# Windowed attention cut into pieces of one 1024-position chunk instead of 342 positions of two chunks

## The chip, the cores and the metric

One core of a Trainium2 chip runs the whole kernel. The engines that matter are TensorE (PE in the profile, with its weight loads as PEld), ScalarE (ACT), VectorE (DVE), GpSimd (POOL), and SyncE (SP), whose queue issues nearly all DMA transfers. Each takes its own instructions in order and waits on semaphores for the others. The metric is the device time of one execution in microseconds.

## What is computed

The input x has 2048 positions of 1024 features; there are 32 heads of 32 features. Two attention blocks read the same x, and a gate per position mixes them.

```python
def _A_ref(x, wqkv, wo):          # linear attention
    ...
    phi = lambda t: jnp.where(t > 0, t + 1, jnp.exp(t)) + 1e-6
    pq, pk = phi(q), phi(k)
    kv = jnp.einsum("bhsd,bhse->bhde", pk, v)
    z = jnp.einsum("bhsd->bhd", pk)
    num = jnp.einsum("bhqd,bhde->bhqe", pq, kv)
    den = jnp.einsum("bhqd,bhd->bhq", pq, z)[..., None] + 1e-6
    o = num / den
    ...
def _B_ref(x, wqkv, wo):          # each position sees itself and 7 earlier ones, 2 apart
    W, dil = 8, 2
    ...
    idx = pos[:, None] - off[None, :]
    mask = idx >= 0
    ...
    logits = jnp.einsum("bhsd,bhswd->bhsw", q, kg) * scale
    logits = jnp.where(mask[None, None, :, :], logits, -1e9)
    attn = _softmax(logits, axis=-1)
    o = jnp.einsum("bhsw,bhswd->bhsd", attn, vg)
    ...
g = _sigmoid((x * gate_w).sum(-1, keepdims=True))
return g * _A_ref(x, A_wqkv, A_wo) + (1 - g) * _B_ref(x, B_wqkv, B_wo)
```

## The kernel before

**Parity.** Attention B steps by 2, so even and odd positions never meet. The kernel keeps them apart: parity p is 0 or 1, each with 1024 positions, and a window of 8 neighbours within its parity.

**Products.** All large matrix products (q, k, v of both blocks and the output projection) use a seven-product scheme in place of eight. The class `Group` computes four output tiles of 128x512 with the products m1 to m7. One product is four matmuls of 512 columns (eight in the output projection). `run` interleaves neighbouring groups: m1 and m2 of the new group, m3 of the one before, m6 of the new, m4 of the one before (`end_of`), then m7 and m5 of the new one. The products m1, m6, m5 and m3 accumulate in one PSUM tile X, one after another. After m1, m6 and m5, ACT saves what X holds so far (`save`, L261: tiles M1s, U2s, U4s), and the next of these products may write X only when that save has read it. The products m2, or m7 and m4, go to a PSUM tile Y; DVE adds the saved tile to it (`acc`, L234) and writes the result (kT, qT, tA, va, vA and so on). X and Y each exist twice, by the parity of the group. That is four PSUM banks.

**Side steps.** The other four banks are one single tile, `side_ps`, tag "s", one buffer. The attention of B (`attn`), the sum kv of block A (`kv`, tile kps) and the last part of A (`qa_out`, tile oA) take turns in it. They are generators: each `yield` gives a delay before the next step of that generator and a number of products for which no other side step may start. `side` counts the products and calls `step`, which takes the next step that is due. PE and SP follow this order as written. The order of ACT and DVE instructions comes out of a scheduler of the framework when the kernel is built; exps, Lns and the copies out of PSUM are marked high priority, and weight sums (L132 to L135) and the sums of phi (L521 to L523) are strewn between products by `defer`.

**Attention B.** For each of four groups of features (nn) and each parity there is one attention, eight in all. A group of features covers two chunks of 128 features (ch 0 and 1), four heads each (g). Positions go in blocks of QB = 57, because a block of 57 and the 7 before it fit in 64 keys. Blocks go in pairs, b = 0 and 1, on partitions 0 to 63 and 64 to 127. A piece t holds three pairs of both chunks, 6 x 57 = 342 columns, and the padded length SPAN is 3 x 342 = 1026. So there are three pieces per attention, 24 in all:

- `scores(t)`: 48 small matmuls (L672) into s, an exp on ACT into PT (L678), and a multiplication by the mask on DVE (L680).
- `pv(t, PT)`: 48 matmuls (L690) with the values and 8 with ones (L696) into o; on ACT, Ln of the row sums into rB (L702) and its exp with -1 (L704), which is the reciprocal; on DVE a copy of the sums into nB (L703) and the product oB (L706). oB is stored to OB_d (L707).

The steps are S0, S1, V0, S2, V1, V2, three products apart. nB and rB have one buffer, oB two. `load_v` reads the values from V_d, where `vb_store` has put them; `out_load` (L778, L781) reads OB_d and OA_d for the output projection.

**Block A beside it.** In the middle of the kernel row groups (`ka_group`, `va_group`) alternate with column groups (`k_group`, `q_group`). In `ka_group`, m3 ends with a cast tA on ACT (L232), followed by the exp eA (L520) and three sums on DVE. After the last kv step KVz is ready, and the queries of A (`qa_plain`, L635) with their oA steps follow.

Of the kernel before, what the change touches and what calls it, by code (L numbers as in the profile page):

```python
# [8 lines left out]
ACT = mybir.ActivationFunctionType  # L9
ALU = mybir.AluOpType  # L10
AX = mybir.AxisListType
BF16 = mybir.dt.bfloat16
FP16 = mybir.dt.float16
F32 = mybir.dt.float32
P = 128
QB = 57
NPAIR = 9
TW = 6 * QB
SPAN = 3 * TW
EPS = 1e-6  # L20
RATE_R = 0.8
OA_DELAY = 5
# [5 lines left out]
def kernel(  # L28
# [27 lines left out]

    consts = ctx.enter_context(tc.tile_pool(name="consts", bufs=1))
    dram = ctx.enter_context(tc.tile_pool(name="dram", bufs=1, space=bass.MemoryType.DRAM))
    V_d = [dram.tile([SPAN, D], BF16, name=f"V_d{p}") for p in range(2)]
    OB_d = [dram.tile([8, P, SPAN], BF16, name=f"OB_d{p}") for p in range(2)]  # L60
    OA_d = [[dram.tile([512, D], BF16, name=f"OA_d{p}{i}") for i in range(2)] for p in range(2)]

    chainp = ctx.enter_context(tc.tile_pool(name="chainp", bufs=5))
# [135 lines left out]

    maskp = consts.tile([P, 2, 6, QB], BF16, name="maskp")
    nc.gpsimd.memset(maskp[:, :, 0, :], 0.0)
    for w in range(8):
        for base in (7 - w, 71 - w):
            nc.gpsimd.affine_select(out=maskp[:, 0, 0, :], in_=maskp[:, 0, 0, :], compare_op=ALU.not_equal,
                                    fill=1.0, base=base, pattern=[[1, QB]], channel_multiplier=-1)
        nc.gpsimd.affine_select(out=maskp[0:64, 1, 0, :], in_=maskp[0:64, 1, 0, :], compare_op=ALU.not_equal,
                                fill=1.0, base=-w, pattern=[[1, QB]], channel_multiplier=-1)
    nc.gpsimd.tensor_copy(out=maskp[64:P, 1, 0, :], in_=maskp[64:P, 0, 0, :])  # L210
    for e in range(1, 6):
        nc.gpsimd.tensor_copy(out=maskp[:, 0, e, :], in_=maskp[:, 0, 0, :])
        nc.gpsimd.tensor_copy(out=maskp[:, 1, e, :], in_=maskp[:, 1 if e == 3 else 0, 0, :])
    ones = consts.tile([P, 32], BF16, name="ones")
    nc.gpsimd.memset(ones[:], 1.0)
    for p in range(2):
        nc.gpsimd.dma_start(out=V_d[p][1024:SPAN, :].rearrange("r (a e) -> (r a) e", e=P), in_=warm[0:16, 0:P])
    bd = consts.tile([P, 4, 33], F32, name="bd")
    nc.gpsimd.memset(bd[:], 0.0)
    for i in range(4):  # L220
# [105 lines left out]
    def col_ops(w, p):  # L326
        return lambda m, kc: (w.get(m, kc), xop(m, kc, p, slice(0, 512)))
# [18 lines left out]
    def step(force=False):  # L346
        seen = set()
        for entry in list(queue):
            if entry[4] in seen:
                continue  # L350
            seen.add(entry[4])
            if not force and (entry[0] > state["now"] or state["free"] > state["now"]):
                continue
            state["free"] = state["now"] + entry[3]
            try:
                delay, entry[3] = next(entry[1])
                entry[0] = state["now"] + delay
# [182 lines left out]
    def va_group(w, pair):  # L540
        vs = v_tiles("vA")

        def kv():
# [18 lines left out]
            if last:  # L562
                nc.vector.tensor_tensor(out=KVz[:].rearrange("p c (g e) -> p c g e", g=4),
                                        in0=KVacc[:, :, None, :].broadcast_to([P, 8, 4, 33]),
                                        in1=bd[:, None, :, :].broadcast_to([P, 8, 4, 33]), op=ALU.mult)
            yield 2, 2

        def done(i):
# [84 lines left out]
            f()  # L653


    def q_of(t, j, b):
        return TW * t + 2 * QB * j + QB * b

    def attn(nn, p, kT, qT, vw):

        def scores(t):
            s = side_ps("s")
            for ch in range(2):
                for j in range(3):
                    e = (3 * ch + j) * QB
                    for b in range(2):
                        q0 = q_of(t, j, b)
                        k0 = max(0, q0 - 7)  # L670
                        for g in range(4):
                            nc.tensor.matmul(s[64 * b:64 * b + 64, g, e:e + QB],  # L672
                                             lhsT=kT[32 * g:32 * g + 32, 1024 * ch + k0:1024 * ch + k0 + 64],
                                             rhs=qT[32 * g:32 * g + 32, 1024 * ch + q0:1024 * ch + q0 + QB],
                                             start=True, stop=True)
            PT = ptp.tile([P, 4, TW], BF16, name="PT", tag="PT")
            with tc.high_priority():
                nc.scalar.activation(out=PT[:], in_=s[:, :, 0:TW], func=ACT.Exp, scale=SCALE)  # L678
            m = maskp[:, 0 if t else 1, :, :].rearrange("p i q -> p (i q)")
            nc.vector.tensor_tensor(out=PT[:], in0=PT[:], in1=m[:, None, :].broadcast_to([P, 4, TW]), op=ALU.mult)  # L680
            return PT

        def pv(t, PT):
            o = side_ps("o")
            for e in range(6):
                ch, j = divmod(e, 3)
                for g in range(4):
                    for b in range(2):
                        rows = slice(64 * b, 64 * b + 64)
                        nc.tensor.matmul(o[32 * g:32 * g + 32, 2 * b, QB * e:QB * e + QB],  # L690
                                         lhsT=vw[rows, 3 * t + j, 4 * ch + g, :],
                                         rhs=PT[rows, g, QB * e:QB * e + QB], start=True, stop=True)
            for g in range(4):
                for b in range(2):
                    rows = slice(64 * b, 64 * b + 64)
                    nc.tensor.matmul(o[32 * g:32 * g + 32, 2 * b + 1, 0:TW], lhsT=ones[rows, :], rhs=PT[rows, g, :],  # L696
                                     start=True, stop=True)
            nB = ofp.tile([P, 2, TW], F32, name="nB", tag="nB", bufs=1)
            rB = ofp.tile([P, 2, TW], F32, name="rB", tag="rB", bufs=1)
            oB = ofp.tile([P, 6, 2, QB], BF16, name="oB", tag="oB", bufs=2)  # L700
            with tc.high_priority():
                nc.scalar.activation(out=rB[:], in_=o[:, 1:4:2, 0:TW], func=ACT.Ln)  # L702
                nc.vector.tensor_copy(out=nB[:], in_=o[:, 0:4:2, 0:TW])  # L703
            nc.scalar.activation(out=rB[:], in_=rB[:], func=ACT.Exp, scale=-1.0)  # L704
            num, r = (ap.rearrange("p b (e q) -> p e b q", e=6) for ap in (nB[:], rB[:]))
            nc.vector.tensor_tensor(out=oB[:], in0=num, in1=r, op=ALU.mult)  # L706
            nc.sync.dma_start(out=OB_d[p][2 * nn:2 * nn + 2, :, TW * t:TW * t + TW].rearrange("c p q -> p c q"),  # L707
                              in_=oB[:].rearrange("p (c j) b q -> p c (j b q)", c=2))

        last = None  # L710
        yield 0, 2
        for t in range(4):
            if t < 3:
                PT = scores(t)
                yield (1, 3) if last else (3, 3)
            if last:
                pv(*last)
                yield 1, 3
            last = (t, PT)

    def load_v(nn, p):
        vw = vwp.tile([P, NPAIR, 8, 32], BF16, name="vw", tag="vw")
        for b, j, n in ((0, 0, 1), (0, 1, 8), (1, 0, 9)):
            k0 = max(0, q_of(0, j, b) - 7)
# [5 lines left out]
    its = {}  # L730

    def k_group(w, nn, p):
        kT = kqp.tile([P, 2050], BF16, name="kT", tag="kq")
        nc.gpsimd.memset(kT[:, 2048:2050], 0.0)
        its[nn, p] = kT
        return Group(col_ops(w, p), lambda i, j, ps, add: acc(kT[:, 1024 * j + 512 * i:1024 * j + 512 * i + 512], ps, add))

    def q_group(w, nn, p):
        qT = kqp.tile([P, 2050], BF16, name="qT", tag="kq")
        nc.gpsimd.memset(qT[:, 2048:2050], 0.0)  # L740
# [5 lines left out]
        return Group(col_ops(w, p), lambda i, j, ps, add: acc(qT[:, 1024 * j + 512 * i:1024 * j + 512 * i + 512], ps, add), done)  # L746


    Wo = {}
# [230 lines left out]
```

## Time and profile before

| What | Value |
|---|---|
| Median of 4 executions | 463.56 us (463.48 to 464.62) |
| Profiled execution, its own time | 464.62 us |
| Its span, first to last instruction | 462.8 us |
| PE busy | 447.3 us (97%) |
| DVE busy | 285.9 us (62%) |
| ACT busy | 241.7 us (52%) |
| First score matmul to last score exp | 68.3 to 290.3 us |
| Exp of a piece (128x1368), 24 times | 1.31 us each |
| Mask product, 24 times | 0.87 us each |
| Ln, reciprocal, nB, oB, 24 times each | 0.74, 0.77, 0.87, 0.87 us each |

The profile lists busy time by engine and, in 40 slices of the span, the busy share in tenths. An instruction's row gives its line, engine, shapes and time. A busy time of PE is modelled from pipelined matmuls; some matmul records are missing, so that a product of four can show as "x3".

### The profile page before, as it was taken

The page shows a single profiled execution, that of the slowest core. Times are in us where ns is not written, and L with a number is a line of the kernel's source. Part 1 is how long each engine was busy: PE and PEld are TensorE (multiplying, and loading weights), DVE is VectorE, ACT ScalarE, POOL GpSimd, SP SyncE. Part 2 cuts the span into 40 slices and gives each one's busy share as a digit, 9 for nine tenths or more (in the row PEclk, how much of TensorE's full clock was granted, in tenths as well). Part 3 has the DMA queues.
Part 4 walks back from the last instruction along what each step waited for, and adds up shares of the span by engine and source line. Part 5 has one row for each costly group of instructions (what it writes and reads, how often), then busy time and mean ns, then how long its engine had stood idle before and what let it go on. Part 6 is the DMA issues. An engine that isn't in the chain of part 4 may idle for free. (4 is left out here: it accounts for less than half of the span.)

```text
span 462.8 us, 11887 instructions
## 1 busy us (share of the span) xinstructions
PE 447.3 (97%) x5060; PEld 218.5 (47%) x5137; DVE 285.9 (62%) x458; ACT 241.7 (52%) x367; POOL 56.7 (12%) x130
## 2 busy tenths in 40 slices
PE   8989999999999999999999999999998999999996
PEld 5435444444444454444444444445544444444444
DVE  0546578668848668486683846579875973154312
ACT  1223337558558485584865858536675645221221
POOL 8000000000000000000000000006675323000000
PEclk9989999999999999999999999999999999999999
DMA  8999721491120612206122065464229972699211
GB/s 178 194 226 237 260 51 64 124 270 25 37 49 18 154 23 57 43 18 144 33 53 48 17 137 175 124 177 113 68 73 202 183 171 79 120 177 182 68 47 45
DMA packets 117941, 51.65 MB, mean 112 GB/s; under 512 B 77696, under 2 KB 115840, under 8 KB 117888
## 3 DMA queue, kind: packets, MB, share of 16 engines
q1 hardware_dynamic: 117520, 50.62, 46.9%
q8 instruction: 40, 0.66, 0.6%
q10 hardware_dynamic: 272, 0.26, 0.2%
q0 software_dynamic: 96, 0.01, 0.1%
q14 instruction: 13, 0.11, 0.1%
HBM read 25.69 MB, written 16.79 MB: 92 GB/s over the span
## 5 line engine op out<-in xcount | busy, mean ns | idle before, releaser
L252 PEld LDWEIGHTS <-xT 128*128 128x128 bf16 (+1 forms) x352 | 32.9, 98 | 38.2 <-issue 1.7
L252 PE MATMUL X<-T,SS 128*128 128x512 f16 x176 | 45.2, 379 | 0.0
L635 PE MATMUL Q<-xT,WS 128*128 128x512 bf16 x185 | 43.0, 379 | 1.1 <-DVE vA L234 0.5
L261 ACT COPY U4s<-X 128x512 f32<-128x512 f32 x40 | 23.2, 581 | 37.3 <-PE X L252 37.2
L252 PEld LDWEIGHTS <-WS 128*128 128x128 bf16 (+1 forms) x288 | 27.0, 98 | 32.9 <-issue 2.5
L678 ACT ACTIVATE PT<-s 128x1368 bf16<-128x1368 f32 x24 | 31.6, 1315 | 19.8 <-PE s L672 19.8
L252 PE MATMUL Y<-W,xT 128*128 128x512 bf16 (+1 forms) x143 | 38.3, 386 | 1.4 <-issue 1.3
L252 PEld LDWEIGHTS <-SS 128*128 128x128 f16 x264 | 24.6, 99 | 28.4 <-issue 1.1
L252 PE MATMUL Y<-xT,WS 128*128 128x512 bf16 (+1 forms) x144 | 37.0, 379 | 0.2 <-DVE qT L234 0.2
L252 PE MATMUL X<-SS,TS 128*128 128x512 f16 x144 | 36.9, 379 | 0.1
L680 DVE TENSOR_TENSOR PT<-PT,maskp 128x1368 bf16<-128x1368 bf16 x24 | 20.8, 868 | 20.8 <-ACT PT L678 20.8
L252 PEld LDWEIGHTS <-TS 128*128 128x128 f16 x216 | 20.5, 98 | 25.2 <-issue 1.8
L261 ACT COPY M1s<-X 128x512 f32<-128x512 f32 x40 | 23.3, 583 | 12.1 <-PE X L252 9.1
L261 ACT COPY U2s<-X 128x512 f32<-128x512 f32 x40 | 23.3, 583 | 10.4 <-PE X L252 10.4
L635 PEld LDWEIGHTS <-WS 128*128 128x128 bf16 x192 | 18.2, 98 | 20.6 <-issue 0.8
L252 PEld LDWEIGHTS <-oT 128*128 128x128 bf16 (+1 forms) x176 | 17.1, 98 | 22.1 <-DMA oT<-OA_d 1.8
L703 DVE COPY nB<-o 128x684 f32<-128x684 f32 x24 | 20.8, 867 | 6.3 <-ACT rB L702 6.0
L603 POOL TENSOR_TENSOR obA<-ofv,rec 128x512 bf16<-128x512 f32 x22 | 24.0, 1110 | 0.9
L640 ACT ACTIVATE eq<-Q 128x512 bf16<-128x512 f32 x24 | 14.3, 598 | 18.4 <-PE Q L635 17.2
L252 PE MATMUL X<-W,SS 128*128 128x512 bf16 x79 | 22.7, 388 | 0.5
L252 PE MATMUL X<-T,oS 128*128 128x512 f16 x96 | 22.7, 379 | 0.0
L252 PE MATMUL Y<-T,xT 128*128 128x512 f16 x88 | 22.6, 379 | 0.0
(137 smaller groups left out, 753.3 us busy)
## 6 DMA issues: line engine op xcount, KB each, us to landing
OB_d<-oB SPq DMA_DIRECT2D x24, 171.0 KB, 3.0
V_d<-va SPq DMA_DIRECT2D x16, 256.0 KB, 2.6
WS<-in_B_wqkv_dram SPq DMA_DIRECT2D x16, 256.0 KB, 4.4
W<-in_A_wqkv_dram SPq DMA_DIRECT2D x8, 512.0 KB, 6.9
OA_d<-obA SPq DMA_DIRECT2D x16, 256.0 KB, 2.4
out_dram<-osb SPq DMA_DIRECT2D x30, 128.0 KB, 1.9
oT<-OB_d SPq DMA_DIRECT2D x12, 256.0 KB, 5.0
vw<-V_d SPq DMA_DIRECT2D x8, 288.0 KB, 5.1
```

What stands on the lines that cost most here:

```text
L252: nc.tensor.matmul(ps[:], lhsT=lhsT, rhs=rhs, start=start and kc == 0, stop=kc == self.nk - 1, skip_group_check=True)
L261: nc.scalar.copy(out=s[:], in_=ps[:])
L603: nc.gpsimd.tensor_tensor(out=ob[:, k:k + 2], in0=of[:, k:k + 2, :, 0:32], in1=rec[:, k:k + 2].broadcast_to([P, 2, 8, 32]), op=ALU.mult)
L635: nc.tensor.matmul(ps[:], lhsT=w.W[:, kc, j * P:j * P + P], rhs=xT[p][:, kc, i, :], start=kc == 0, stop=kc == 7, skip_group_check=True)
L640: nc.scalar.activation(out=es[i][:, j, :], in_=ps[:], func=ACT.Exp)
L678: nc.scalar.activation(out=PT[:], in_=s[:, :, 0:TW], func=ACT.Exp, scale=SCALE)
L680: nc.vector.tensor_tensor(out=PT[:], in0=PT[:], in1=m[:, None, :].broadcast_to([P, 4, TW]), op=ALU.mult)
L703: nc.vector.tensor_copy(out=nB[:], in_=o[:, 0:4:2, 0:TW])
```

## The change

A piece now is one chunk with all 1024 positions of the parity. Eight pairs of blocks of 57 and one pair of 56 make 2 x 512 positions, so a piece fills 512 columns, one whole bank, for each of the four heads. There are two pieces per attention, 16 in all, with 72 + 72 block matmuls and 8 row sums of 512 columns each. exp and mask work on 2048 elements per partition, Ln, its exp and nB on 1024; oB is computed in two instructions (912 and 112), and has one buffer instead of two. The steps are S0, S1, V0, V1, in the built kernel 4, 4 and 3 products apart. One mask of 512 columns replaces the two of 342; the padding of V_d, kT and qT goes; `load_v` issues four transfers instead of three. An oA step may start only after KVz has been written.

```diff
@@ step
+            if entry[4] == "oa" and "KVz" not in ready:
+                continue
...
+    def block(j, b):
+        q0 = 2 * QB * j + (QB if j < 8 else QB - 1) * b
+        return q0, QB if j < 8 else QB - 1, min(max(0, q0 - 7), 960)
...
@@ attn
-        def scores(t):
+        def scores(ch):
             s = side_ps("s")
-            for ch in range(2):
-                for j in range(3):
-                    e = (3 * ch + j) * QB
-                    for b in range(2):
-                        q0 = q_of(t, j, b)
-                        k0 = max(0, q0 - 7)
-                        for g in range(4):
-                            nc.tensor.matmul(s[64 * b:64 * b + 64, g, e:e + QB],
...
+            for j in range(NPAIR):
+                for b in range(2):
+                    q0, n, k0 = block(j, b)
+                    for g in range(4):
+                        nc.tensor.matmul(s[64 * b:64 * b + 64, g, QB * j:QB * j + n],
+                                         lhsT=kT[32 * g:32 * g + 32, ch, k0:k0 + 64],
+                                         rhs=qT[32 * g:32 * g + 32, ch, q0:q0 + n], start=True, stop=True)
-            PT = ptp.tile([P, 4, TW], BF16, name="PT", tag="PT")
+            PT = ptp.tile([P, 4, 512], BF16, name="PT", tag="PT")
             with tc.high_priority():
-                nc.scalar.activation(out=PT[:], in_=s[:, :, 0:TW], func=ACT.Exp, scale=SCALE)
+                nc.scalar.activation(out=PT[:], in_=s[:], func=ACT.Exp, scale=SCALE)
...
-            nB = ofp.tile([P, 2, TW], F32, name="nB", tag="nB", bufs=1)
-            rB = ofp.tile([P, 2, TW], F32, name="rB", tag="rB", bufs=1)
-            oB = ofp.tile([P, 6, 2, QB], BF16, name="oB", tag="oB", bufs=2)
+            nB = ofp.tile([P, 2, 512], F32, name="nB", tag="nB", bufs=1)
+            rB = ofp.tile([P, 2, 512], F32, name="rB", tag="rB", bufs=1)
+            oB = ofp.tile([P, 1024], BF16, name="oB", tag="oB", bufs=1)
...
-            nc.vector.tensor_tensor(out=oB[:], in0=num, in1=r, op=ALU.mult)
+            nc.vector.tensor_tensor(out=oB[:, 0:2 * n].rearrange("p (j b q) -> p j b q", j=8, b=2), in0=num, in1=r,
+                                    op=ALU.mult)
+            nc.vector.tensor_tensor(out=oB[:, 2 * n:1024].rearrange("p (b q) -> p b q", b=2), in0=nB[:, :, n:512],
+                                    in1=rB[:, :, n:512], op=ALU.mult)
+            nc.sync.dma_start(out=OB_d[p][2 * nn + ch, :, :], in_=oB[:])
-        last = None
-        yield 0, 2
-        for t in range(4):
-            if t < 3:
-                PT = scores(t)
-                yield (1, 3) if last else (3, 3)
-            if last:
-                pv(*last)
-                yield 1, 3
-            last = (t, PT)
+        yield 0, 4
+        PT = [scores(0)]
+        yield 1, 4
+        PT.append(scores(1))
+        for ch in range(2):
+            yield 1, 3
+            pv(ch, PT[ch])
+        yield 1, 3
@@ load_v
-        for b, j, n in ((0, 0, 1), (0, 1, 8), (1, 0, 9)):
+        for b, j, n in ((0, 0, 1), (0, 1, 8), (1, 0, 8), (1, 8, 1)):
@@ k_group, q_group (the same for qT)
-        kT = kqp.tile([P, 2050], BF16, name="kT", tag="kq")
-        nc.gpsimd.memset(kT[:, 2048:2050], 0.0)
+        kT = kqp.tile([P, 2, 1024], BF16, name="kT", tag="kq")
```

More of the change, by code (lines that the diff above doesn't have):

```diff
@@ L17 @@
 NPAIR = 9
-TW = 6 * QB
-SPAN = 3 * TW
 EPS = 1e-6
@@ L58 @@
     dram = ctx.enter_context(tc.tile_pool(name="dram", bufs=1, space=bass.MemoryType.DRAM))
-    V_d = [dram.tile([SPAN, D], BF16, name=f"V_d{p}") for p in range(2)]
-    OB_d = [dram.tile([8, P, SPAN], BF16, name=f"OB_d{p}") for p in range(2)]
+    V_d = [dram.tile([1024, D], BF16, name=f"V_d{p}") for p in range(2)]
+    OB_d = [dram.tile([8, P, 1024], BF16, name=f"OB_d{p}") for p in range(2)]
     OA_d = [[dram.tile([512, D], BF16, name=f"OA_d{p}{i}") for i in range(2)] for p in range(2)]
@@ L198, in x_loads, with diagonal @@
                 xt_load(tile_of(pair, i))
-    maskp = consts.tile([P, 2, 6, QB], BF16, name="maskp")
-    nc.gpsimd.memset(maskp[:, :, 0, :], 0.0)
-    for w in range(8):
[L205 to L213, printed above, removed]
+    maskp = consts.tile([P, 512], BF16, name="maskp")
+    nc.gpsimd.memset(maskp[:], 0.0)
+    def diagonal(cols, base):
+        nc.gpsimd.affine_select(out=maskp[:, cols], in_=maskp[:, cols], compare_op=ALU.not_equal, fill=1.0,
+                                base=base, pattern=[[1, cols.stop - cols.start]], channel_multiplier=-1)
+    for w in range(8):
+        diagonal(slice(0, QB), -w)
+        diagonal(slice(QB, 2 * QB), 7 - w)
+        diagonal(slice(QB, 2 * QB), 71 - w)
+        diagonal(slice(8 * QB, 512), 72 - w)
+    for j in range(2, 8):
+        nc.gpsimd.tensor_copy(out=maskp[:, QB * j:QB * j + QB], in_=maskp[:, QB:2 * QB])
+    nc.gpsimd.tensor_copy(out=maskp[64:P, 0:QB], in_=maskp[64:P, QB:2 * QB])
+    nc.gpsimd.tensor_copy(out=maskp[0:64, 8 * QB:512], in_=maskp[0:64, QB:2 * QB - 1])
     ones = consts.tile([P, 32], BF16, name="ones")
     nc.gpsimd.memset(ones[:], 1.0)
-    for p in range(2):
-        nc.gpsimd.dma_start(out=V_d[p][1024:SPAN, :].rearrange("r (a e) -> (r a) e", e=P), in_=warm[0:16, 0:P])
     bd = consts.tile([P, 4, 33], F32, name="bd")
@@ L565, in kv @@
                                         in1=bd[:, None, :, :].broadcast_to([P, 8, 4, 33]), op=ALU.mult)
+                ready.add("KVz")
             yield 2, 2
@@ L653, in qa_plain @@
             f()
-    def q_of(t, j, b):
-        return TW * t + 2 * QB * j + QB * b
+    def block(j, b):
+        q0 = 2 * QB * j + (QB if j < 8 else QB - 1) * b
+        return q0, QB if j < 8 else QB - 1, min(max(0, q0 - 7), 960)
     def attn(nn, p, kT, qT, vw):
-        def scores(t):
+        def scores(ch):
             s = side_ps("s")
-            for ch in range(2):
-                for j in range(3):
-                    e = (3 * ch + j) * QB
-                    for b in range(2):
-                        q0 = q_of(t, j, b)
-                        k0 = max(0, q0 - 7)
-                        for g in range(4):
[L672 to L675, printed above, removed]
-            PT = ptp.tile([P, 4, TW], BF16, name="PT", tag="PT")
+            for j in range(NPAIR):
[6 more added lines that the diff above has]
+            PT = ptp.tile([P, 4, 512], BF16, name="PT", tag="PT")
@@ L677, in scores @@
             with tc.high_priority():
-                nc.scalar.activation(out=PT[:], in_=s[:, :, 0:TW], func=ACT.Exp, scale=SCALE)
-            m = maskp[:, 0 if t else 1, :, :].rearrange("p i q -> p (i q)")
-            nc.vector.tensor_tensor(out=PT[:], in0=PT[:], in1=m[:, None, :].broadcast_to([P, 4, TW]), op=ALU.mult)
+                nc.scalar.activation(out=PT[:], in_=s[:], func=ACT.Exp, scale=SCALE)
+            nc.vector.tensor_tensor(out=PT[:], in0=PT[:], in1=maskp[:, None, :].broadcast_to([P, 4, 512]), op=ALU.mult)
@@ L681, in scores, with pv @@
             return PT
-        def pv(t, PT):
+        def pv(ch, PT):
             o = side_ps("o")
-            for e in range(6):
-                ch, j = divmod(e, 3)
+            for j in range(NPAIR):
+                cols = slice(QB * j, QB * j + block(j, 0)[1])
                 for g in range(4):
@@ L689, in pv @@
                         rows = slice(64 * b, 64 * b + 64)
-                        nc.tensor.matmul(o[32 * g:32 * g + 32, 2 * b, QB * e:QB * e + QB],
-                                         lhsT=vw[rows, 3 * t + j, 4 * ch + g, :],
-                                         rhs=PT[rows, g, QB * e:QB * e + QB], start=True, stop=True)
+                        nc.tensor.matmul(o[32 * g:32 * g + 32, 2 * b, cols], lhsT=vw[rows, j, 4 * ch + g, :],
+                                         rhs=PT[rows, g, cols], start=True, stop=True)
             for g in range(4):
@@ L695, in pv @@
                     rows = slice(64 * b, 64 * b + 64)
-                    nc.tensor.matmul(o[32 * g:32 * g + 32, 2 * b + 1, 0:TW], lhsT=ones[rows, :], rhs=PT[rows, g, :],
+                    nc.tensor.matmul(o[32 * g:32 * g + 32, 2 * b + 1, :], lhsT=ones[rows, :], rhs=PT[rows, g, :],
                                      start=True, stop=True)
-            nB = ofp.tile([P, 2, TW], F32, name="nB", tag="nB", bufs=1)
-            rB = ofp.tile([P, 2, TW], F32, name="rB", tag="rB", bufs=1)
-            oB = ofp.tile([P, 6, 2, QB], BF16, name="oB", tag="oB", bufs=2)
+            nB = ofp.tile([P, 2, 512], F32, name="nB", tag="nB", bufs=1)
@@ L701, in pv @@
+            rB = ofp.tile([P, 2, 512], F32, name="rB", tag="rB", bufs=1)
+            oB = ofp.tile([P, 1024], BF16, name="oB", tag="oB", bufs=1)
             with tc.high_priority():
-                nc.scalar.activation(out=rB[:], in_=o[:, 1:4:2, 0:TW], func=ACT.Ln)
-                nc.vector.tensor_copy(out=nB[:], in_=o[:, 0:4:2, 0:TW])
+                nc.scalar.activation(out=rB[:], in_=o[:, 1:4:2, :], func=ACT.Ln)
+                nc.vector.tensor_copy(out=nB[:], in_=o[:, 0:4:2, :])
             nc.scalar.activation(out=rB[:], in_=rB[:], func=ACT.Exp, scale=-1.0)
-            num, r = (ap.rearrange("p b (e q) -> p e b q", e=6) for ap in (nB[:], rB[:]))
@@ L706, in pv @@
-            nc.vector.tensor_tensor(out=oB[:], in0=num, in1=r, op=ALU.mult)
-            nc.sync.dma_start(out=OB_d[p][2 * nn:2 * nn + 2, :, TW * t:TW * t + TW].rearrange("c p q -> p c q"),
-                              in_=oB[:].rearrange("p (c j) b q -> p c (j b q)", c=2))
-        last = None
-        yield 0, 2
-        for t in range(4):
-            if t < 3:
-                PT = scores(t)
-                yield (1, 3) if last else (3, 3)
-            if last:
-                pv(*last)
-                yield 1, 3
-            last = (t, PT)
+            n = 8 * QB
@@ new lines, in pv @@
+            num, r = (ap[:, :, 0:n].rearrange("p b (j q) -> p j b q", j=8) for ap in (nB, rB))
+            nc.vector.tensor_tensor(out=oB[:, 0:2 * n].rearrange("p (j b q) -> p j b q", j=8, b=2), in0=num, in1=r,
[3 more added lines that the diff above has]
+            nc.sync.dma_start(out=OB_d[p][2 * nn + ch, :, :], in_=oB[:])
@@ L721, in load_v @@
+        yield 0, 4
[6 more added lines that the diff above has]
+        yield 1, 3
     def load_v(nn, p):
         vw = vwp.tile([P, NPAIR, 8, 32], BF16, name="vw", tag="vw")
-        for b, j, n in ((0, 0, 1), (0, 1, 8), (1, 0, 9)):
-            k0 = max(0, q_of(0, j, b) - 7)
+        for b, j, n in ((0, 0, 1), (0, 1, 8), (1, 0, 8), (1, 8, 1)):
+            k0 = block(j, b)[2]
             src = cols_of(V_d[p][k0:k0 + 64, :], nn)
@@ L732, in k_group @@
     def k_group(w, nn, p):
-        kT = kqp.tile([P, 2050], BF16, name="kT", tag="kq")
-        nc.gpsimd.memset(kT[:, 2048:2050], 0.0)
+        kT = kqp.tile([P, 2, 1024], BF16, name="kT", tag="kq")
         its[nn, p] = kT
-        return Group(col_ops(w, p), lambda i, j, ps, add: acc(kT[:, 1024 * j + 512 * i:1024 * j + 512 * i + 512], ps, add))
+        return Group(col_ops(w, p), lambda i, j, ps, add: acc(kT[:, j, 512 * i:512 * i + 512], ps, add))
     def q_group(w, nn, p):
-        qT = kqp.tile([P, 2050], BF16, name="qT", tag="kq")
-        nc.gpsimd.memset(qT[:, 2048:2050], 0.0)
+        qT = kqp.tile([P, 2, 1024], BF16, name="qT", tag="kq")
         vw = load_v(nn, p)
@@ L745, in done @@
                 add_side(2, attn(nn, p, its[nn, p], qT, vw), p, "attn")
-        return Group(col_ops(w, p), lambda i, j, ps, add: acc(qT[:, 1024 * j + 512 * i:1024 * j + 512 * i + 512], ps, add), done)
+        return Group(col_ops(w, p), lambda i, j, ps, add: acc(qT[:, j, 512 * i:512 * i + 512], ps, add), done)
     Wo = {}
```

## The prediction

> **What bounds the kernel now.** I read the page from the top: busy shares, then the slices.
>
> ```profile
> span 462.8 us, 11887 instructions
> PE 447.3 (97%) x5060; PEld 218.5 (47%) x5137; DVE 285.9 (62%) x458; ACT 241.7 (52%) x367; POOL 56.7 (12%) x130
> ...
> PE   8989999999999999999999999999998999999996
> ...
> DVE  0546578668848668486683846579875973154312
> ACT  1223337558558485584865858536675645221221
> ...
> PEclk9989999999999999999999999999999999999999
> ```
>
> TensorE (PE) is busy 97% and its clock is nearly full throughout, so time can only come from work taken off TensorE or from idle there, 15.5 us in all. ScalarE (ACT) and VectorE (DVE) are half idle on average, but their rows swing between 4 and 8 in slices 6 to 25, which are the attention stage. That is where to look for the gaps between bursts. Dividing that stage at the first score matmul of successive attentions:
>
> ```profile
> 102.59:132.87 30.28, 28.96 (x482) 13.92 (x489) 23.73 (x36) 19.11 (x27) 0.68 (x4) 1.00 0.25 52
> 132.87:161.98 29.11, 28.48 (x482) 13.85 (x488) 20.01 (x32) 19.11 (x27) 0.65 (x4) 1.00 0.29 69
> ```
>
> (window, its length, then busy time of PE, PEld, DVE, ACT, POOL, granted clock, DMA.) A period is 28 products, six attention steps and one kv step. One attention from the timeline (start, length):
>
> ```profile
> 136.06 0.57 PE L672 MATMUL s<-qT,kT 32*64 32x57 bf16 x48
> 136.56 1.04 PE L252 MATMUL X<-W,SS 128*128 128x512 bf16 x3
> 136.70 1.31 ACT L678 ACTIVATE PT<-s 128x1368 bf16<-128x1368 f32 x1 [0.81 <-PE s L672]
> 137.91 0.58 ACT L232 CAST tA<-X 128x512 bf16<-128x512 f32 x1
> ...
> 138.52 1.06 ACT L520 ACTIVATE eA<-tA 128x1024 bf16<-128x1024 bf16 x1
> 139.26 0.54 PE L690 MATMUL o<-PT,vw 64*32 64x57 bf16 x48
> ...
> 139.49 0.57 ACT L261 COPY U2s<-X 128x512 f32<-128x512 f32 x1
> 139.61 0.37 PE L696 MATMUL o<-PT,ones 64*32 64x342 bf16 x8
> 139.92 1.04 PE L252 MATMUL Y<-xT,WS 128*128 128x512 f16 x4
> ...
> 140.79 1.03 PE L252 MATMUL X<-SS,TS 128*128 128x512 f16 x4
> ...
> 141.81 0.87 DVE L703 COPY nB<-o 128x684 f32<-128x684 f32 x1
> ```
>
> Between its steps TensorE runs products 0.865 us apart (139.92 to 140.79). The X product at 140.79 overwrites an accumulator that ACT finishes saving (U2s) at 140.06: 0.7 us to spare, behind an exp, a cast and another exp. The copy nB is what frees the single four-bank PSUM tile for the next attention step.
>
> **What the change does, part by part.**
>
> TensorE. A score step costs 0.10 (gap at entry) + 0.50 (136.06 to 136.56) = 0.60 us. Its 48 matmuls issue within 0.38 us, the busy 0.57 less the last one's own 0.19, or 8.1 ns each; 0.12 is the exit. 72 take 0.58, the step 0.80. A value step costs 0.10 + 0.35 (48 blocks) + 0.31 (8 row sums) = 0.76. With 72 blocks (0.53) and row sums of 512 columns instead of 342 (170 columns more, at the 0.216 us that 512 take in a product: +0.07, as the eight run beside one another) it costs 1.01. 24 pairs x 1.36 = 32.6; 16 pairs x 1.81 = 29.0. **-3.6 us**, all on the bound engine. Bounds: -1.6 (only the entry gaps of 16 steps go and the rest scales) to -4.
>
> [...]
>
> ACT and DVE. Sizes come from rows that straddle the new ones. ACT: a 512 copy takes 0.58, the 1368 exp 1.31, so 0.85 ns per element: exp of 2048 is 1.89 us, Ln of 1024 (between 684 at 0.74 and the 1056 copy at 1.04) 1.02, the reciprocal's Exp 1.06 (as eA, 1024). DVE: the 2048-element bf16 weight sum takes 1.22, which I take for the mask; nB (684: 0.87; 512: 0.69; 1.04 ns per element) becomes 1.22; the product oB 1.10 + 0.27. Their totals hardly move and neither engine is the bound, so the totals count nothing. The length of each piece counts, because both queues run in order.
>
> [...] The rows show 0.14 us fixed per ACT instruction, so eight exps, Lns and reciprocals fewer save 3.4 us of ACT. [...]
>
> Stall A, U2s. The steps now stand at products 0, 4, 8 and 11 of an attention, instead of 0, 3, 6, 9, 12 and 15. The built kernel's ACT order has changed with that: the second score step comes after product m3, so cast tA and exp eA stand ahead of its exp, and U2s behind all three. I walk an attention from its first score matmul: products start at 0.70, 1.57, 2.43, 3.30; second scores 4.26 to 4.96; products at 4.96, 5.82, 6.69, and m5, the one that needs U2s, at 7.55. ACT takes an X 0.20 after its product (U2s at 131.25, next product 131.05): tA 4.36 to 4.94, eA to 6.00. The exp could start at 5.10, starts at 5.9 (ACT overlaps its neighbours by 0.1) and ends at 7.8; U2s 7.7 to 8.3. m5 waits 0.8. Seven of the eight attentions have this order; the first has no eA and no wait. 7 x 0.8 = **+5.6**. Bounds 0.4 and 1.0 each.
>
> Stall B, nB. After m5 (8.35 to 9.21) the first value step ends at 10.2, three products follow, and the second wants the PSUM tile at 12.9. The built kernel's DVE order is then: add U2s (8.35 to 9.03), mask (to 10.2), and then, ahead of nB, in four attentions eA add, tA max, kT add, eA min, eA add (0.69 + 0.42 + 0.69 + 0.42 + 0.69, less overlaps of 0.08, to 12.7). nB ends at 13.95: wait 1.1. In two, four small weight sums (0.43) and one add stand there: 0.7. In the second attention a 1.22 us sum too: 1.3. In the first (no A, one 1.22 us sum and one add): 0.2. 4 x 1.1 + 2 x 0.7 + 1.3 + 0.2 = **+7.3**. Bounds: 3 (0.5 less each) and 11.
>
> After that rB, nB and oB have one buffer each: the second Ln waits for the first oB (15.8), U2s stands behind it and ends at 17.3, against its product at 17.5; DVE's adds to kT (19.3) and vA (21) are level with theirs. I book nothing, but there is no cover left.
>
> Waits of now that go. The 30.28 us period is 1.2 us over the ordinary one. The trace gives this:
>
> ```profile
> DVE nB L703 <- ACT rB L702: 6.0, 8, 1.6
> ...
> 112.97 0.56 PE L672 MATMUL s<-qT,kT 32*64 32x57 bf16 x48 [0.56 <-DVE nB L703]
> ```
>
> Those gaps belong to its third score step and value steps, which are gone. The other periods are 0.1 over the sum of their steps. 1.2 + 7 x 0.1 = **-1.9**.
>
> The end. The linear part's oA steps come one product earlier (the last kv step is at product 274, not 275). In the trace the last oA of parity 0 (338.80) is followed at once by another (340.60), 0.45 us late; then its store holds SP's queue and the OA_d transposes, and the first output product waits 1.30 us for them (352.38). One product more of room is worth 0.45 and some 0.4 of the 1.30: **-0.9** (0 to -1.7).
>
> Nothing else reaches TensorE. The mask on POOL is ready by 12 us now, and first needed near 70. SP issues 8 fewer OB_d stores and 8 more vw loads, at 0.4 to 0.6 us; the loads go out some 10 us ahead. The POOL memsets and pads leave an engine that is 12% busy. The KVz guard orders the program and costs no instruction.
>
> Sum: -3.6 + 5.6 + 7.3 - 1.9 - 0.9 = +6.5 us. The profiled execution took 464.62 (span 462.8 and 1.8 around it), 1.06 over the median; 471.1 by its own measure, **470.1** by the median.
>
> **Rivals.**
>
> 1. The bursts fit (faster). Tile orders with real slack would show both stalls near zero: then -3.6 - 1.9 - 0.9 = -6.4, 457.2 us. For it: ACT 52%, DVE 62%, and 3 to 4 products of room after each step. Against it: A and B are queues of named instructions, not totals. It decides if the stalls, 12.9 together, come out at under half: exp on ACT by 5.1 rather than 5.9 and nB on DVE a microsecond earlier.
> 2. The single buffers bind (slower still). The second oB waits until the store of the first has landed: median 3.0 us now, 4.3 the longest. At 4.3 every accumulator behind it is some 0.8 late: 8 x 0.8 = +6.4, 476.5.
> 3. One stall only. A gone: 464.5; B gone: 462.8. Fewer steps against one stall is then about no change.
>
> **How the numbers follow.** The forecast has 0.54, its own range 465 to 474. Rival 2 has 0.18, rival 1 0.16, rival 3 0.12, split between faster, same and slower. A measurement here can tell about 0.2%, 0.9 us, from no change. Faster 0.20, same 0.05, slower 0.75. The range 461 to 476 leaves out most of rival 1 and the top of rival 2, no more than 2 in 10.
>
> **What would show it.** Right: in the waits, PE X L252 behind ACT for some 0.8 in seven attentions, and PE o behind DVE nB about 1 us in each; periods of 30 to 30.5 us (28 x 0.865, one kv step at 0.72, two score and two value steps, and the waits); 16 exps of 1.9 us; TensorE's busy time 3 to 4 us down. Wrong: periods of 28.5 us (rival 1), or a DVE wait for the OB_d store (rival 2). A score step over 0.9 us would take the first term away.

## The result, and the profile after

The changed kernel takes 463.28 us (median of 53 executions, 462.28 to 465.58); the kernel before took 464.11 beside it (79 executions, 462.68 to 467.17). The ratio is 0.9982, 95% interval 0.9974 to 0.9989: 0.8 us faster (0.5 to 1.2), about 0.2%. The prediction said 6.5 us slower. The time lies in its range, the sign is wrong.

In some executions of every kernel here TensorE's mean granted clock is 0.996 or less instead of 0.998 to 1.000 and the time 1.5 to 2.3 us longer, so "at full clock" below means the median over the executions at 0.998 or more (3 to 8 of each experiment, none of e4): 463.4 to 463.7 before, 463.06 after.

The page of after, first and second part:

```profile
span 460.9 us, 11711 instructions
...
PE 443.9 (96%) x5019; PEld 217.5 (47%) x5073; DVE 282.4 (61%) x450; ACT 235.8 (51%) x343; POOL 59.4 (13%) x117
...
PE   7989999998999999999999999999999999999996
...
PEclk9999999999999999999999999999999999999999
```

The span is 1.9 us shorter than that of before, more than the kernels differ: before's trace holds a fall of the clock near 31 us (last section). TensorE's busy time is 3.4 us down, and the prediction asked for 3 to 4, but this agreement is chance. Ahead of the first score matmul, where the change has no step, it is 2.5 us down (64.87 and 62.36), and there before's clock fell (mean 0.98 up to that matmul, against 1.00 in after). Behind it, it is only 0.8 down (382.40 and 381.57). Busy time is modelled, with records missing, so what the steps save is better read from the periods below. What TensorE does with the room shows when the stage is cut at the first score matmuls again (window, length, busy time of PE, PEld, DVE, ACT, POOL, clock, DMA):

```profile
100.62:130.60 29.98, 28.58 (x477) 13.84 (x480) 23.47 (x35) 18.54 (x24) 0.48 (x2) 1.00 0.22 53
130.60:159.97 29.37, 28.44 (x477) 13.77 (x481) 19.35 (x31) 18.51 (x24) 0.48 (x2) 1.00 0.30 68
```

The ordinary period is 29.4 us: not the 30 to 30.5 of the forecast, nor the 28.5 of rival 1. The waits say which stall it is (engine, what it waited for, total, times, longest):

```profile
PE X L252 <- ACT U2s L261: 4.5, 7, 0.7
...
PE o L689 <- DVE nB L701: 0.6, 1, 0.6
```

Stall A is there in seven attentions; stall B in one, the second (29.98 us). The attention that starts at 130.60, on the timeline:

```profile
128.98 0.59 ACT L261 COPY U2s<-X 128x512 f32<-128x512 f32 x1 [0.28 <-PE X L252]
...
134.97 0.59 ACT L232 CAST tA<-X 128x512 bf16<-128x512 f32 x1 [0.68 <-PE X L252]
135.58 1.06 ACT L522 ACTIVATE eA<-tA 128x1024 bf16<-128x1024 bf16 x1
136.55 1.86 ACT L678 ACTIVATE PT<-s 128x2048 bf16<-128x2048 f32 x1
137.50 0.69 DVE L234 TENSOR_TENSOR tA<-Y,U2s 128x512 bf16<-128x512 f32 x1
138.30 0.58 ACT L261 COPY U2s<-X 128x512 f32<-128x512 f32 x1
138.44 1.23 DVE L679 TENSOR_TENSOR PT<-PT,maskp 128x2048 bf16<-128x2048 bf16 x1 [0.25 <-ACT PT L678]
138.93 1.02 PE L252 MATMUL X<-SS,TS 128*128 128x512 f16 x4 [0.61 <-ACT U2s L261]
...
142.28 1.22 DVE L701 COPY nB<-o 128x1024 f32<-128x1024 f32 x1
...
143.55 0.74 PE L689 MATMUL o<-PT,vw 64*32 64x57 bf16 x72
```

Cast, exp eA, score exp and U2s stand on ACT in the order that was foreseen, and the product at 138.93 comes 0.77 us late (the next free place was 138.16, 0.865 after 137.30). But look at DVE: the add "tA<-Y,U2s" runs at 137.50, *before* the U2s of this group is saved at 138.30. It reads the U2s saved for the group before, at 128.98. So the mask starts with the end of the exp, at 138.44, and nB ends at 143.50, just before the second value step starts at 143.55.

Dividing both traces at the first scores of the first and of the eighth attention: between them 210.15 us before, 210.95 after (+0.80); from the eighth to the end 184.38 before, 183.23 after (-1.15). In the stage the change loses a little; at the end it gains more.

### The profile page after: what moved, and what is told of

It is laid out like the page before. It is cut to its first block, busy times and chain, and to the rows that moved or that the text cites. A ratio compares the mean times of both kernels' runs of the same rounds, so it can differ in the third digit from the quotient of the medians.

```text
span 460.9 us, 11711 instructions
## 1 busy us (share of the span) xinstructions
PE 443.9 (96%) x5019; PEld 217.5 (47%) x5073; DVE 282.4 (61%) x450; ACT 235.8 (51%) x343; POOL 59.4 (13%) x117
## 4 chain that ended last, share of the span: by engine, by line
PE 85%; ACT 6%; DMA 3%; SPq 3%; issue 1%; DVE 1%; ACTq 0%; DVEq 0%
PE X L252 38%; PE Y L252 26%; PE Q L638 9%; PE K L497 3%; ACT PT L678 3%; PE o L689 2%; ACT eA L522 2%; PE oA L595 1%; PE s L673 1%; SPq L778 1%; DMA W<-in_B_wqkv_dram 1%; PE kps L556 1%; DMA oT<-OA_d 1%; ACT tA L232 1%; PE o L694 1%
## 5 line engine op out<-in xcount | busy, mean ns | idle before, releaser
L252 PEld LDWEIGHTS <-WS 128*128 128x128 bf16 (+1 forms) x288 | 28.1, 98 | 33.6
L463 POOL MEMSET vA<- 128x32 bf16 x16 | 4.0, 250 | 271.5 <-DVE eA L525 144.7
L678 ACT ACTIVATE PT<-s 128x2048 bf16<-128x2048 f32 x16 | 29.9, 1869 | 15.1 <-PE s L673 15.0
L679 DVE TENSOR_TENSOR PT<-PT,maskp 128x2048 bf16<-128x2048 bf16 x16 | 19.6, 1224 | 22.1 <-ACT PT L678 22.1
L606 POOL TENSOR_TENSOR obA<-ofv,rec 128x512 bf16<-128x512 f32 x22 | 25.7, 1187 | 0.9
L701 DVE COPY nB<-o 128x1024 f32<-128x1024 f32 x16 | 19.5, 1220 | 6.0 <-ACT rB L700 6.0
L700 ACT ACTIVATE rB<-o 128x1024 f32<-128x1024 f32 x16 | 16.4, 1025 | 12.2 <-DVE oB L707 9.4
```

The costliest lines, as they stand in the source:

```text
L252: nc.tensor.matmul(ps[:], lhsT=lhsT, rhs=rhs, start=start and kc == 0, stop=kc == self.nk - 1, skip_group_check=True)
L606: nc.gpsimd.tensor_tensor(out=ob[:, k:k + 2], in0=of[:, k:k + 2, :, 0:32], in1=rec[:, k:k + 2].broadcast_to([P, 2, 8, 32]), op=ALU.mult)
L678: nc.scalar.activation(out=PT[:], in_=s[:], func=ACT.Exp, scale=SCALE)
L679: nc.vector.tensor_tensor(out=PT[:], in0=PT[:], in1=maskp[:, None, :].broadcast_to([P, 4, 512]), op=ALU.mult)
L700: nc.scalar.activation(out=rB[:], in_=o[:, 1:4:2, :], func=ACT.Ln)
L701: nc.vector.tensor_copy(out=nB[:], in_=o[:, 0:4:2, :])
```

## The experiments

Four questions: does stall A cost what it seems to; is nB really without room; where does the gain at the end come from; and what would the change be without its stalls.

### Moving one step or one exp: e1, e2

The first moves the second score step one product nearer, so that its exp stands ahead of cast and eA again:

```diff
-        yield 0, 4
+        yield 0, 3
```

> The changed kernel (463.3 us), with the second score step 3 products after the first instead of 4, so that its exp stands ahead of the cast tA and the exp eA on ACT again. Theory T (the wait of m5 for U2s, 0.61 to 0.67 us of idle and 0.77 to 0.83 us of delay in seven attentions, is what eats the saving on TensorE): those waits go, 5.5 us are saved, less up to 0.2 us per attention where Ln now stands behind two eA: 458 to 459.5 us. Rival R (TensorE would wait just as long one step later, for the PSUM tile or for DVE): 462 to 463.5 us, with new waits of 0.6 us or more at the value steps.

Measured: 466.38 us against 464.47, ratio 1.0039 (1.0018 to 1.006). Theory T failed. The long wait for U2s is gone, but the periods did not shrink: 29.02 and 29.72 in turn, because others took its place.

```profile
PE o L689 <- issue: 2.3, 1, 2.3
PE Y L252 <- DVE kT L234: 1.8, 3, 0.7
PE X L252 <- ACT U2s L261: 1.4, 5, 0.3
...
PE o L689 <- DVE nB L701: 1.1, 1, 1.1
```

The first of these is no engine's: in the eighth attention TensorE stopped in the middle of a value step, and the products behind it took 1.89 and 1.73 us instead of 1.03:

```profile
292.99 0.22 PE L689 MATMUL o<-PT,vw 64*32 64x56 bf16 x7 [2.31 <-issue]
293.01 0.54 PE L694 MATMUL o<-PT,ones 64*32 64x512 bf16 x8
293.49 1.89 PE L252 MATMUL X<-W,SS 128*128 128x512 bf16 x4
295.17 1.73 PE L252 MATMUL X<-T,SS 128*128 128x512 f16 x4
```

The second leaves the steps where they are and holds the exp eA of the first row tile on ACT until the second score exp has been issued. The three sums on DVE that follow this exp start two products later too:

```diff
-            defer(0, phi(e[:], ts[i][:]))
+            if i == 0:
+                def first():
+                    with tc.issue_after(pt["exp"]) if pt["exp"] else nullcontext():
+                        nc.scalar.activation(out=e[:], in_=ts[0][:], func=ACT.Exp)
+                later(2, first)
+                defer(2, phi(e[:], ts[0][:], False))
...
-                nc.scalar.activation(out=PT[:], in_=s[:], func=ACT.Exp, scale=SCALE)
+                pt["exp"] = nc.scalar.activation(out=PT[:], in_=s[:], func=ACT.Exp, scale=SCALE).ins
```

> The changed kernel with the steps where they are, and only one thing moved: the exp eA of the first row of a ka group is issued on ACT behind the second score exp instead of ahead of it. Theory T: the second score exp starts at 5.1 instead of 5.9 us after the first score matmul, U2s ends at 7.5, level with m5 at 7.55: seven waits of 0.8 us go, 457.5 to 459 us. Rival Q (the longer exp of 2048 by itself is enough to delay U2s): the waits stay at 0.4 us or more, 460.5 to 463 us. Rival R (the wait moves on to the value steps): 462 to 463.5 us.

Measured: 461.99 against 464.47, ratio 0.9929 (0.9898 to 0.996); at full clock 459.97, 3.1 us below the changed kernel, less than expected. All seven waits for U2s are gone, and a wait that the changed kernel had once is there seven times:

```profile
PE o L698 <- DVE nB L710: 2.9, 7, 1.0
```

In the attention that starts at 132.21 it looks like this:

```profile
143.51 1.22 DVE L710 COPY nB<-o 128x1024 f32<-128x1024 f32 x1
...
144.78 0.74 PE L698 MATMUL o<-PT,vw 64*32 64x57 bf16 x72 [0.36 <-DVE nB L710]
```

Of the 5.6 us that stall A costs (7 x 0.8), 2.3 come back as nB (2.9 less the 0.6 of the changed kernel). In this attention the second value step wants the tile 0.8 us earlier than in the changed kernel, while nB ends only 0.4 earlier (12.5 us after the first score matmul instead of 12.9). The moved sums are not the reason: from the end of the mask to the start of nB it is 2.6 us in both. The delay of stall A had been cover for nB.

### nB's room, tested from the other side: e4

```diff
                 nc.vector.tensor_copy(out=nB[:], in_=o[:, 0:4:2, :])
+                nc.vector.tensor_copy(out=nB[:], in_=o[:, 0:4:2, :])
```

> The changed kernel with the copy nB out of PSUM done twice (1.22 us and the add that stands between the two more before the PSUM tile is free). Theory T (in the changed kernel nB ends level with the second value step, 143.50 against 143.55 us, with no room at all): the second value step waits 1.2 to 1.9 us in each of eight attentions, 473 to 478 us. Rival (nB has a microsecond of room, and the prediction was wrong in size by that much): under 5 us slower, at most 468 us.

Measured: 477.77 against 464.47, ratio 1.0289 (1.0267 to 1.0311).

```profile
PE o L689 <- DVE nB L702: 13.4, 8, 2.3
PE X L252 <- ACT U2s L261: 4.5, 7, 0.7
```

One copy of 1.22 us more, and the add of 0.68 that stands behind nB (143.41 in after), became 1.4 to 2.3 us of wait in each of the eight, with stall A unchanged. nB ends level with the step that wants its PSUM tile, and nothing is left over.

### Both stalls, two by two: e5, e8

If the two share one budget, both cures together give more than the sum of each alone. e8 is the changed kernel with value steps four products apart instead of three; e5 is e2 with the same edit:

```diff
-            yield 1, 3
+            yield 1, 4
             pv(ch, PT[ch])
```

> The changed kernel with only this edit: the two value steps 4 products apart instead of 3, eA where the change has it. Theory T2: the wait for U2s covers nB already, so only the one wait of 0.58 us in the second attention goes: 462.3 to 463.3 us, no more than 1 us under the changed kernel. Rival (nB, not U2s, is what holds the changed kernel back): 2 to 3 us faster, 460 to 461 us.

> The kernel with eA behind the second score exp (460.3 us of span, 462.0 median) and, besides, the two value steps 4 products apart instead of 3. Theory T2 (in the changed kernel the wait for U2s and the room for nB are one budget: the 0.8 us that TensorE waits for U2s are 0.8 us of cover for DVE, so taking that wait away uncovers waits for nB of 0.2 to 1.0 us, 2.9 us in all): with one product more of room the nB waits go and the seven U2s waits stay away, 2.5 to 3 us under the kernel it is made from, 458.5 to 459.5 median. Rival (nB's wait only moves to a later accumulator, kT or vA, through the single buffers of rB and nB): within 0.8 us of the kernel it is made from.

Measured: e8 462.34, ratio 0.9967 (0.9949 to 0.9985); e5 457.16 against 464.60, ratio 0.985 (0.9824 to 0.9876), below its range, which had been reckoned from e2's median of 462.0 (at full clock e5 is 2.9 below e2, as expected). At full clock, with the changed kernel at 463.06:

| | values 3 apart | values 4 apart |
|---|---|---|
| eA ahead of the second score exp | 463.06 (after) | 462.25 (e8) |
| eA behind it | 459.97 (e2) | 457.09 (e5) |

The single cures give 0.8 and 3.1, both together 6.0: more than the 3.9 of their sum, as one budget wants it. In e5 neither wait is left, and the period is

```profile
157.99:186.56 28.57, 28.15 (x477) 13.80 (x480) 19.09 (x31) 18.45 (x24) 0.48 (x2) 1.00 0.20 49
```

This is the bare sum of the steps as the prediction costed them: 28 x 0.865 + 0.72 + 2 x 0.80 + 2 x 1.01 = 28.56.

### The stop in the eighth attention: e6, e7

While TensorE stood in e1, four loads of 512 KB each (A's output weights, issued together at 283.88) had filled the DMA engines: 97% busy in the 5 us to 290. In e6 (made from e5) and e7 (made from e1) they are issued four products apart:

```diff
-                nc.sync.dma_start(out=W[:, 4 * i:4 * i + 4, 512 * j:512 * j + 512],
...
+                def load(i=i, j=j):
+                    nc.sync.dma_start(out=W[:, 4 * i:4 * i + 4, 512 * j:512 * j + 512],
...
+                if gap:
+                    later(gap * (2 * j + i), load)
...
-        Wo[k] = row_weights(src, 0)
+        Wo[k] = row_weights(src, 0, 4 if k == "A" else 0)
```

> The kernel with both edits (eA behind the score exp, value steps 4 apart), and the four loads of A_wo, 512 KB each, issued 4 products apart instead of at once. Theory F (in the eighth attention the second value step stands still for 0.2 to 2.3 us waiting for nothing in the program, in every version of the changed kernel, while those four loads keep all 16 DMA engines full and an instruction transfer is late behind them): the stop is under 0.2 us, 0.3 to 1 us faster than with both edits alone. Rival (the stop has nothing to do with the loads): still there, same time within 0.3.

> The changed kernel with the score steps 3 products apart (466.4 us median, a stop of 2.31 us at 292 us and slow products after it) and the four loads of A_wo spread over 12 products. Theory F: the stop of 2.3 us goes, and with it the two products of 1.9 and 1.7 us that followed it instead of 1.03 each: 2.5 to 4 us faster, 462.5 to 464 us. Rival: the stop stays, 466 us.

Measured: e6 456.36 against 464.60, ratio 0.9835 (0.9805 to 0.9865), **the fastest version here**; e7 464.24, ratio 0.9985 (0.9964 to 1.0005), a smaller gain than expected. The stop is in neither trace (2.31 us in e1, 0.80 in e5). At full clock e7 is 2.2 us below e1, e6 1.0 below e5. So in these traces the stop comes only with the loads issued together; they do not suffice, since before issues them together too (DMA share 1.00 from 285 to 290) and has no such stop, and neither has e4. How it comes about is not shown, and the late instruction transfer of e6's expectation is not either. The rest of e1's loss is its moved waits: e7 still has the kT, U2s and nB lines of e1.

### Where the end's gain comes from: e3, e9, e10

The prediction put it on the oA steps. e3 is the changed kernel with the first eight oA steps held back to where they were before:

```diff
-            if entry[4] == "oa" and "KVz" not in ready:
+            if entry[4] == "oa" and ("KVz" not in ready or state["now"] < state["kvz"] + 6):
```

> The changed kernel with the first eight oA steps of block A held back by one product, at the products where the kernel before has them. Theory T (the shorter attention lets them start one product earlier, which takes 0.45 us at the ninth oA step and part of the 1.3 us wait for the transposes of OA_d): both waits come back, 0.5 to 1.5 us slower, 463.8 to 464.8 us. Rival: the end is bound by products and not by these waits, 463.3 us within 0.3.

Measured: 463.67, ratio 0.9991 (0.9973 to 1.0009), less than expected; at full clock 463.43, 0.4 above the changed kernel. The wait at the ninth oA came back (0.32 us), but the 1.30 us wait of the first output product for the OA_d transposes did not. In before the two look like this:

```profile
340.60 0.62 PE L592 MATMUL oA<-KVz,eq 128*128 128x132 bf16 x8 [0.32 <-ACT ofv L594]
...
352.38 1.90 PE L252 MATMUL X<-W,oT 128*128 128x512 bf16 x7 [1.30 <-DMA oT<-OA_d]
```

Something else in the change had removed the second. One line was left that the prediction had passed over, and that the diff above leaves out: with the padding, the rows of OB_d in DRAM go from 1026 to 1024 elements (2052 to 2048 bytes). e9 gives the changed kernel the old pitch, e10 gives the kernel before a pitch of 1088 (2176 bytes, as its pieces need 1026):

```diff
-    OB_d = [dram.tile([8, P, 1024], BF16, name=f"OB_d{p}") for p in range(2)]
+    OB_d = [dram.tile([8, P, 1026], BF16, name=f"OB_d{p}") for p in range(2)]
...
-    OB_d = [dram.tile([8, P, SPAN], BF16, name=f"OB_d{p}") for p in range(2)]
+    OB_d = [dram.tile([8, P, 1088], BF16, name=f"OB_d{p}") for p in range(2)]
```

> The changed kernel with one thing put back: the rows of OB_d are 1026 elements apart again (2052 bytes) instead of 1024 (2048 bytes); the same bytes are moved. Theory P (part of the time that the change takes from the end comes from this pitch and not from the oA order: with the old oA order but the new pitch the wait of 1.30 us for the transposes did not come back): loads of OB_d land after 5.0 us again instead of 4.1, SP needs 1.9 instead of 1.2 us for a pair of them, TensorE waits for the transposes of OA_d for up to 1.3 us, 0.3 to 1.3 us slower than the changed kernel, 463.6 to 464.6 us. Rival (the pitch has nothing to do with it): loads at 4.1 us, same time within 0.3.

> The kernel before with only this edit: the rows of OB_d 1088 elements apart (2176 bytes, a multiple of 128) instead of 1026. Theory P: its loads of OB_d land after about 4.1 us instead of 5.0, SP's pair takes 1.2 us, and the wait of 1.30 us for the transposes shrinks or goes: 0.4 to 1.3 us faster than the kernel before. Rival: no difference that can be measured.

Measured: e9 465.62 against 464.25, ratio 1.0038 (1.0017 to 1.006), a larger loss than expected; e10 462.55 against 464.25, ratio 0.9968 (0.995 to 0.9986), a larger gain than expected. At full clock:

| | pitch 1026 | pitch 1024 or 1088 |
|---|---|---|
| pieces of 342, two chunks | 463.60 (before) | 462.09 (e10) |
| pieces of 1024, one chunk | 465.57 (e9) | 463.06 (after) |

Read down a column: the pieces alone cost 1 to 2 us. Read along a row: the pitch alone gives 1.5 to 2.5. The trace of e9 shows the place, first its SP queue, then its TensorE:

```profile
345.02 1.17 SPq L775 DMA_DIRECT2D oT<-OB_d  x2
346.30 5.64 SPq L778 DMA_TRANSPOSE oT<-OA_d  x2
```

```profile
353.49 2.92 PE L252 MATMUL X<-W,oT 128*128 128x512 bf16 x7 [2.41 <-DMA oT<-OA_d]
```

and the changed kernel the same rows without the wait:

```profile
343.83 1.17 SPq L775 DMA_DIRECT2D oT<-OB_d  x2
345.10 3.46 SPq L778 DMA_TRANSPOSE oT<-OA_d  x2
```

The first pair of OB_d loads holds SP for 1.17 us in both, not the 1.9 expected for e9. The transposes are issued behind these loads. With rows of 2052 bytes such a load lands in a median 5.0 to 5.1 us (before and e9), with 2048 or 2176 in 4.1 (after and e10), and the transposes, 5.64 against 3.46, end that much later. In e10 the wait for them is gone while the 0.32 us at the ninth oA stays: the exact opposite of putting the oA steps back. The pitch does not decide this wait alone: e5 and e8, with rows of 2048 bytes, have 0.6 and 0.5 us of it.

## Why the prediction failed, step by step

| Term | Predicted, us | Measured, us |
|---|---|---|
| TensorE's steps | -3.6 | -3.4 (16 pairs of 0.80 + 1.03 for 24 of 1.36) |
| Stall A, U2s | +5.6 | +5.5 (7 x 0.77 to 0.83) |
| Stall B, nB | +7.3 | +0.6 (one wait) |
| Waits of now | -1.9 | not measured apart; the periods agree |
| The end | -0.9 | -1.75 of waits gone (0.45 and 1.30) |

**The steps were right.** A score step takes 0.80 (130.60 to 131.30, and 0.10 at entry), a value step 1.03 against 1.01 (e5, 166.41 to 167.44); the exp of 2048 takes 1.87 us against 1.89, mask and nB 1.22 as booked. e5's period closes this sum to 0.01 us.

**Stall A was right** in place, number and size.

**Stall B is the step that failed.** The prediction walked DVE's queue on the clock of the attention as "add U2s (8.35 to 9.03), mask (to 10.2)", and so had nB end at 13.95 against 12.9. It took the add for one that must wait for the U2s that stall A delays. That add belongs to m4 of the group *before*, whose U2s had been saved a group earlier; after the first score matmul of its attention it runs at 6.9 and the mask from 7.8 to 9.1. Everything behind it comes 1.1 us earlier, and nB ends at 12.9. The other side of the comparison was right: the second value step, with A's 0.8 already in its time, was put at 12.9 and stands at 12.95. So A was not counted twice; it was let delay DVE too, and with it nB. In the trace A delays TensorE and hardly DVE, so its 0.8 us cover nB, and e2 and the table of e5 and e8 show that: take A away and B appears. With 0.6 in place of 7.3 the prediction's own sum would be -0.2. That nB's end and the step meet within 0.05 us is chance: nothing in the change aims at it.

**The end had about the right size and the wrong cause.** The oA order is worth 0.3 to 0.45 us. The 1.30 us for the transposes, of which the prediction booked 0.4 to oA's "one product more of room", went with the row pitch of OB_d, a line that was read as padding with no cost. Without it the changed kernel would be 2 us slower than before (e9), so the sign of the piece-wise argument was right, and its size was three to seven times too large.

**Rivals.** Rival 1 (the bursts fit, 457.2) came true only in part as built: nB is a microsecond earlier and the two stalls come to 6.1 of 12.9 us, just under the half that it named, but the exp still starts at 5.9 and the time is 6 us above. e5 and e6 (457.16 and 456.36) show that the rest can be met by two or three edits; their agreement with 457.2 is partly chance, since they hold the pitch's gain, which the rival did not know. Rival 2 (single buffers) did not happen: the store of OB_d lands in 2.1 us, not 4.3, and DVE never waits for it. In e9, with the old pitch, the store takes 3.0 us; but DVE's waits for it do not follow the pitch alone: e5 and e8, with rows of 2048 bytes, have 1.4 and 0.8 us of them. Rival 3 ("B gone: 462.8") came nearest, and stall B is indeed all but gone; that its time fits so well is partly the pitch again.

**What the sum leaves open.** Steps, stalls and waits as measured, with the -1.9 as booked, add up to -1.0; the two traces, from the first score matmul on, differ by -0.35, and the medians by 0.8. The rest is of the size of single small stops (after has one of 0.18 us in the eighth attention), and where it lies stays open.

## What to carry to other kernels

When stalls on different engines follow from one edit, put them on one clock: a delay of the bound engine (here 0.8 us per attention) is cover for every queue that it does not delay, so curing one stall can uncover another, and cures are tested in pairs (each alone, and both). The step that failed here was a smaller one: which group's tile an instruction reads. Before an add or a copy is placed in a queue, settle that, since in a software pipeline the neighbour's is a whole group older. And read every line of a diff that changes the layout of a DRAM tensor: here four bytes of row pitch decided the sign (at full clock 465.57 with 2052 bytes, 463.06 with 2048, 463.60 before).

## What the hardware showed that had not been expected

**Row pitch.** Rows of 2052 bytes against 2048 or 2176: loads of 256 KB 5.0 to 5.1 us against 4.1; stores of 256 KB 3.0 (e9) against 2.1 (after), while stores of 171 KB hardly gain, 3.0 (before, 2052) against 2.9 (e10, 2176). These loads read 256 bytes per row. The runs hold three pitches, of which 2048 and 2176 give the same 4.1 us; why 2052 is slower they do not show.

**The granted clock can fall after short waits.** In the profile of before TensorE waits 0.79 and 0.71 us for xT near 29 us, a little apart, and two products later the matmuls are slow; in after, with 0.28 and 0.99, they are not:

```profile
28.62 0.35 PE L442 MATMUL gps<-gw,xT 128*128 128x1 bf16 x8 [0.79 <-DMA xT<-in_A_x_dram]
29.68 0.35 PE L442 MATMUL gps<-gw,xT 128*128 128x1 bf16 x8 [0.71 <-DMA xT<-in_A_x_dram]
...
31.09 1.91 PE L252 MATMUL Y<-W,xT 128*128 128x512 bf16 x4 [0.22 <-issue]
32.80 1.53 PE L252 MATMUL X<-W,SS 128*128 128x512 bf16 x4
```

The same follows e1's stop of 2.31 us (products of 1.89 and 1.73, clock 0.82 in the 5 us around it) and e9's wait of 2.41 us (clock 0.91 from 340 to 360), but not before's single wait of 1.30 us at 352. In these three traces the slow matmuls took 1.4 to 1.6 us more than such matmuls elsewhere (before 1.91 and 1.53 instead of 1.03 each, e1 1.89 and 1.73 instead of 1.03 each, e9 2.92 and 1.08 instead of the 1.90 and 0.62 of before). The length of the waits alone does not decide: after 0.79 and 0.71 us before's matmuls were slow, after 0.21 and 1.36 us e3's were not; after a single wait of 1.78 us e2's products took 1.86 and 1.91, after one of 1.49 us e4's took 1.02 and 1.03. What else decides stays open.
